# Pooling scores by column tiles, turned by VectorE's block transposes, in a fused attention and maxout kernel

## The chip, the cores and the metric

One core of one Trainium2 chip. The metric is the device time of one execution in microseconds (us). The six runs of the changed kernel lie within 0.2% (341.00 to 341.64 us); the kernel before spreads more (337.8 to 341.4 us over all sessions), and the first experiment says why. Engines: PE is TensorE's matmuls, PEld its weight loads, DVE VectorE, ACT ScalarE, POOL GpSimd, SP the sync engine.

## The reference, cut to what matters

```python
B, N, m, C = 4, 12544, 32, 128
def mab(q, kv):                                  # attention, one head
    s = q @ kv.transpose(0, 2, 1) / sqrt(C)
    a = exp(s - max(s)); a /= a.sum(-1) + 1e-9
    return a @ kv
h = mab(inducing, x)                             # pooling: 32 queries over 12544 rows
y = mab(x, h)                                    # 12544 queries over 32 rows
g = maximum(y @ w1, y @ w2)                      # maxout, 1024 wide
out = g @ w_out
```

A batch has 98 chunks of 128 rows. The pooling of batch b+1 is woven into the main loop of batch b; the first batch's is done at the start.

## The kernel before

The main loop has 196 steps, 49 a batch. A **slot** is one step: a *burst* of row-tiled matmuls into four PSUM banks (L564), their four relus on ScalarE (L599) and VectorE (L595), the 16 output matmuls (L626) of an earlier burst, and the multiply by the softmax denominators on VectorE (L652, called *o*). The program deals its PSUM tiles out to eight banks, and each tile waits for its bank to be read out (in the window of batch 1 shown in the prediction the second L579 matmul starts at 154.71 us, 0.05 us after the last relu of the burst before it has ended). A small cost model in the program picks the engine of each relu. In every other slot, four small matmuls (L579) go ahead into two more banks. `stage` computes the exp of the second attention's scores of a block.

Pooling of the next batch's block i (16 chunks, the seventh has 2):

```python
def p1_scores(b, i):                       # L324: one matmul per chunk, rows in the partitions
    for j in range(n):
        nc.tensor.matmul(out=ps[:, j*M:(j+1)*M], lhsT=xT_tiles[b % 2][:, k0 + j, :],
                         rhs=inducingT, start=True, stop=True)
    nc.scalar.activation(out=et[:, 0:n, :], in_=ps[:, 0:n*M], func=AF.Exp, scale=scale)

def p1_accum(b, i):                        # L346: pooling; the sums of E go to GpSimd
    for j in range(n):
        nc.tensor.matmul(out=ps[:, 0:M], lhsT=xn[:, j, :], rhs=et[:, j, :], ...)
    nc.vector.tensor_add(out=hacc, in0=ps[:, 0:M], in1=hacc)
    nc.gpsimd.tensor_add(out=eacc, in0=eacc, in1=et[:, 0:n, :])

def small_fold(b): ...                     # GpSimd: eacc folded to 32 columns, 4 adds
def small_h(b): ...                        # TensorE sums eacc over partitions, then h
```

The schedule, and the order within a slot:

```python
for i in range(NP1):
    s = g + (14 + 4*i if b == 0 else 5 + 5*i)
    at(s, p1_scores, nb, i)
    at(s + 2, p1_accum, nb, i)
    if nb + 1 < B: at(g + l0 + 2*i, load_x, nb + 1, i)
d = 1 if b == 0 else 0
for s, f in ((40, small_fold), (42, small_h), (43, small_hwd), (44, small_m1)):
    at(g + s + (0 if f is small_fold else d), f, nb)
...
for g, (p, u) in enumerate(seq):
    p.burst(u, lead)
    for blk in stages.get(g, ()): blk.stage()
    if queue: part.final(*a)               # output matmuls, o, and a transfer in every other slot
    for f, *a in jobs.pop(g, ()): f(*a)    # pooling's scores, sums, loads
```

The softmax here doesn't subtract the row's maximum and nothing guards it: scores larger than these inputs give would overflow.

## Time and profile before

| | kernel before |
|---|---|
| time, six runs beside the changed kernel | median 338.86 us (338.05 to 340.41) |
| first profile | span 337.9 us, clock 0.994 |
| PE, DVE, ACT busy | 98%, 88%, 80% |
| plain slot, slot with L579 | 1.329, 1.441 us |
| slot with scores or with pooling | +0.391, +0.390 us |

The slot lengths are the differences between the starts of successive bursts in the timeline of TensorE; nearly all of them repeat to a few ns from execution to execution (a plain slot: 1.328 to 1.330 us; the odd ones are named where they matter), so two kernels can be compared slot by slot. The page's lines that matter are shown and read in the prediction below.

### The profile page before, as it was taken

What the parts mean: (1) busy time and instruction counts of PE and PEld (TensorE: products, weight loads), DVE (VectorE), ACT (ScalarE), POOL (GpSimd) and SP (SyncE); (2) the same over time, 40 slices, a digit from 0 to 9 for tenths busy, and PEclk for the clock granted to TensorE, in tenths of its full rate; (3) what the DMA queues carried; (4) which work ended last, traced back from release to release, by engine and by line L of the source; (5) the groups of instructions that cost most, each with busy time, mean ns of one, the idle gap of its engine ahead of it and who ended that gap; (6) DMA issues with size and microseconds to landing.
All of it is one profiled execution on the core that took longest, in us unless ns stands there. A gap on an engine that the chain in (4) does not pass through costs nothing.

```text
span 337.9 us, 14526 instructions
## 1 busy us (share of the span) xinstructions
PE 330.4 (98%) x6352; PEld 263.9 (78%) x6352; DVE 297.1 (88%) x628; ACT 271.6 (80%) x523; POOL 94.6 (28%) x166
## 2 busy tenths in 40 slices
PE   8999999999999999999999999999999999999995
PEld 3876678888878878888777878888777777878875
DVE  1558999999989999999998999999998998999993
ACT  3748988777898887787898877787899989888881
POOL 6242112275641234543341232332242100000000
PEclk9989999999999999999999999999999999999999
DMA  8999699999929996995229991221221221222222
GB/s 213 209 207 214 171 196 227 196 241 253 262 80 206 222 208 150 175 251 156 79 85 174 258 222 65 97 91 68 96 96 66 108 98 68 95 94 95 96 97 109
DMA packets 54143, 51.47 MB, mean 152 GB/s; under 512 B 41536, under 2 KB 42464, under 8 KB 54080
## 3 DMA queue, kind: packets, MB, share of 16 engines
q0 software_dynamic: 11552, 32.38, 37.6%
q1 hardware_dynamic: 42528, 18.17, 25.4%
q8 instruction: 49, 0.80, 1.0%
q14 instruction: 14, 0.11, 0.1%
HBM read 28.33 MB, written 25.69 MB: 160 GB/s over the span
## 4 chain that ended last, share of the span: by engine, by line
PE 92%; DMA 3%; ACT 2%; DVE 1%; issue 1%; POOL 1%; POOLq 0%
PE ps L626 57%; PE ps L564 19%; PE ps L579 4%; DMA xn<-in_x_dram 3%; PE ps L324 2%; PE ps L346 2%; PE ps L499 2%; ACT relu L599 2%; PE ps L210 1%; PE ps L260 1%; DVE o L652 1%; PE ps L226 1%; PE ps L520 1%; DVE relu L595 1%; PE ps L408 1%
## 5 line engine op out<-in xcount | busy, mean ns | idle before, releaser
L599 ACT ACTIVATE relu<-ps 128x512 f16<-128x512 f32 x445 | 236.0, 601 | 42.1 <-PE ps L564 30.2
L595 DVE TENSOR_SCALAR relu<-ps 128x512 f16<-128x512 f32 x339 | 218.1, 679 | 5.0 <-PE ps L564 4.0
L626 PE MATMUL ps<-woutp,relu 128*128 128x128 f16 x3136 | 208.6, 220 | 0.0
L626 PEld LDWEIGHTS <-relu 128*128 128x128 f16 x3136 | 175.7, 98 | 31.3 <-issue 21.6
L652 DVE TENSOR_TENSOR o<-ps,rp 128x256 f32<-128x256 f32 x196 | 81.8, 417 | 16.3 <-PE ps L626 11.6
L662 POOL DMA_DIRECT2D out_dram<-o x75 | 41.3, 551 | 150.1 <-DVE o L652 102.6
L564 PE MATMUL ps<-e,hwd 32*128 32x256 f16 (+1 forms) x1632 | 82.5, 269 | 0.7 <-ACT relu L599 0.2
L564 PEld LDWEIGHTS <-hwd 32*128 32x128 f16 x1632 | 27.0, 92 | 19.2 <-issue 3.7
L579 PE MATMUL ps<-m,e 32*128 32x128 f16 x372 | 29.8, 214 | 0.8
L579 PEld LDWEIGHTS <-e 32*128 32x128 f16 x372 | 18.3, 92 | 7.1 <-issue 4.2
L366 POOL TENSOR_TENSOR eacc<-eacc,et 128x512 f32<-128x512 f32 (+1 forms) x18 | 18.5, 1029 | 0.3
L333 ACT ACTIVATE et<-ps 128x512 f16<-128x512 f32 (+1 forms) x21 | 11.4, 545 | 5.0 <-PE ps L324 5.0
L120 POOL DMA_DIRECT2D xn<-in_x_dram x21 | 11.4, 545 | 4.9 <-DMA xn<-in_x_dram 1.7
L509 ACT ACTIVATE e<-ps 128x512 f16<-128x512 f32 (+1 forms) x21 | 10.9, 578 | 0.0
L324 PE MATMUL ps<-inducingT,xT 128*128 128x32 f16 x294 | 10.6, 176 | 0.2 <-ACT relu L599 0.2
L346 PE MATMUL ps<-et,xn 128*128 128x32 f16 x294 | 10.6, 176 | 0.0
L215 DVE COPY xT<-ps 128x1024 f16<-128x1024 f16 (+2 forms) x10 | 5.8, 596 | 5.2 <-PE ps L210 5.1
L324 PEld LDWEIGHTS <-xT 128*128 128x128 f16 x294 | 9.5, 96 | 0.4 <-issue 0.4
L346 PEld LDWEIGHTS <-xn 128*128 128x128 f16 x294 | 9.5, 96 | 0.0
L191 PE MATMUL ps<-warm 128*128 128x512 f16 x22 | 7.8, 502 | 1.2 <-DVE warm L167 1.2
L499 PE MATMUL ps<-xT,hT 128*32 128x512 f16 (+2 forms) x120 | 8.8, 353 | 0.0
L210 PE MATMUL ps<-identity,xn 128*128 128x128 f16 x98 | 7.1, 219 | 0.6 <-DMA xn<-in_x_dram 0.3
(79 smaller groups left out, 123.6 us busy)
## 6 DMA issues: line engine op xcount, KB each, us to landing
out_dram<-o POOLq DMA_DIRECT2D x72, 256.0 KB, 3.9
xn<-in_x_dram POOLq DMA_DIRECT2D x21, 512.0 KB, 9.3
out_dram<-o SPq DMA_DIRECT2D x24, 256.0 KB, 2.0
xf<-in_x_dram SPq DMA_DIRECT2D x2, 512.0 KB, 4.2
wf<-in_moe_w_dram SPq DMA_DIRECT2D x2, 512.0 KB, 6.8
xn<-in_x_dram POOLq DMA_DIRECT2D x3, 256.0 KB, 12.0
out_dram<-o POOLq DMA_DIRECT2D x3, 128.0 KB, 4.6
xT<-xn SPq DMA_TRANSPOSE x21, 6.9
```

What stands on the lines that cost most here:

```text
L120: nc.gpsimd.dma_start(out=xn_of(b, i)[:, 0:n, :], in_=xr[b, :, k0 : k0 + n, :])
L324: nc.tensor.matmul(out=ps[:, j * M : (j + 1) * M], lhsT=xT_tiles[b % 2][:, k0 + j, :], rhs=inducingT, start=True, stop=True,)
L346: nc.tensor.matmul(out=ps[:, 0:M], lhsT=xn[:, j, :], rhs=et[:, j, :], start=(j == 0), stop=(j == n - 1),)
L366: nc.gpsimd.tensor_add(out=acc, in0=acc, in1=et[:, 0:n, :])
L499: nc.tensor.matmul(out=ps[32 * q : 32 * (q + 1), 0 : self.width], lhsT=st[self.b]["hT4"][:, 32 * q : 32 * (q + 1)], rhs=xT[:, q % self.g], ...
L564: nc.tensor.matmul(out=ps[:, jj * w : (jj + 1) * w], lhsT=st[blk.b]["hwd"][r, 128 * jb : 128 * (jb + 1)], rhs=blk.e2[r, 128 * self.t0 : 12 ...
L579: nc.tensor.matmul(out=part.fin[q][1][:, 128 * s : 128 * (s + 1)], lhsT=part.blk.e2[r, 128 * tt : 128 * (tt + 1)], rhs=st[part.blk.b]["m1" ...
L595: nc.vector.tensor_scalar(out=dst, in0=src, scalar1=0.0, scalar2=None, op0=ALU.max)
L599: nc.scalar.activation(out=dst, in_=src, func=AF.Relu)
L626: nc.tensor.matmul(out=o, lhsT=self.relu[:, jb, q, tt, :], rhs=woutp[:, jb, :], start=(start and s == 0 and jb == 0), stop=(not start and ...
L652: nc.vector.tensor_mul(self.osb[:, h : h + 2, :], ps[:, 0:256].rearrange("p (s c) -> p s c", s=2), rp.broadcast_to((128, 2, 128)),)
L662: eng.dma_start(out=outr[blk.b, :, k : k + nst, :], in_=self.osb[:, 0:nst, :])
```

## The change

Intent: score a block with four matmuls into four column tiles, side by side (the four L499 matmuls of a round start within 10 ns of each other in the first profile of before, the next round 0.227 us later), in place of 16; do it ahead of the output matmuls so that its exp falls into the lengthened slot; bring E back to rows in the partitions by turning each block of 32 queries by 32 rows on VectorE (one instruction, 0.70 us for 128x512 in the profile after); give turn, pooling and the small steps one slot more; spread a batch's loads over more slots; and finish the start with its smallest unit. The core of the diff:

```diff
+        def col_scores(b, k0, n, name):
+            bi, ps = bank([128, P1B * M])
+            for q in range(4):
+                r = slice(32 * q, 32 * (q + 1))
+                nc.tensor.matmul(out=ps[r, 0 : n * 32], lhsT=inducingT,
+                    rhs=xT_tiles[b % 2][:, k0 : k0 + n, r],
+                    start=True, stop=True, tile_position=(0, 32 * q))
+            eT = eTp.tile([128, P1B * M], F16, name=f"eT_{name}", tag="eT")
+            nc.scalar.activation(out=eT[:, 0 : n * M], in_=ps[:, 0 : n * M], func=AF.Exp, scale=scale)
+            return eT, model.bank_free[bi]
+        def col_turn(eT, ready, n, name):
+            et = etp.tile([128, P1B, M], F16, name=f"et_{name}", tag="et")
+            nc.vector.transpose(et[:, 0:n, :].rearrange("p k m -> p (k m)"), eT[:, 0 : n * M])
+            return et, model.ev("DVE", n * M, ready)
 ... (the start: units 0 to 2 of batch 0 use both; last units in natural order)
-                at(s, p1_scores, nb, i)
-                at(s + 2, p1_accum, nb, i)
+                scores.setdefault(s, []).append((nb, i))
+                at(s + 2, p1_turn, nb, i)
+                at(s + 3, p1_accum, nb, i)
-                    at(g + l0 + 2 * i, load_x, nb + 1, i)
-            d = 1 if b == 0 else 0
-            for s, f in ((40, small_fold), (42, small_h), (43, small_hwd), (44, small_m1)):
-                at(g + s + (0 if f is small_fold else d), f, nb)
+                    at(g + l0 + 3 * i, load_x, nb + 1, i)
+            for s, f in ((41, small_fold), (43, small_h), (44, small_hwd), (45, small_m1)):
+                at(g + s, f, nb)
 ...
                 blk.stage()
+            for b, i in scores.get(g, ()):
+                p1_scores(b, i)
             if queue:
```

"Batch 1", "batch 2" below name the stretch of the main loop (49 slots, counted from 0); the pooling in it is that of the next batch. (The prediction, in "first score of batch 1" and the like, and the expectations name the batch that is pooled; the schedule's slot numbers are the same.)

More of the change, by code (lines that the diff above doesn't have):

```diff
@@ L82 @@
             units.append((i, 0, n))
-    units = units[:-4] + units[-1:] + units[-4:-1]
     NU = len(units)
@@ L89 @@
     etp = ctx.enter_context(tc.tile_pool(name="etp", bufs=7))
+    eTp = ctx.enter_context(tc.tile_pool(name="eTp", bufs=3))
     e2p = ctx.enter_context(tc.tile_pool(name="e2p", bufs=5))
@@ L196 @@
         st = [dict() for _ in range(B)]
+        def col_scores(b, k0, n, name):
+            bi, ps = bank([128, P1B * M])
+            for q in range(4):
+                r = slice(32 * q, 32 * (q + 1))
+                nc.tensor.matmul(
+                    out=ps[r, 0 : n * 32],
+                    lhsT=inducingT,
+                    rhs=xT_tiles[b % 2][:, k0 : k0 + n, r],
+                    start=True,
+                    stop=True,
+                    tile_position=(0, 32 * q),
+                )
+            end = model.pe(32 * n / 2400, model.bank_free[bi], "col")
+            eT = eTp.tile([128, P1B * M], F16, name=f"eT_{name}", tag="eT")
+            nc.scalar.activation(
+                out=eT[:, 0 : n * M], in_=ps[:, 0 : n * M], func=AF.Exp, scale=scale
+            )
+            model.bank_free[bi] = model.ev("ACT", n * M, end)
+            return eT, model.bank_free[bi]
+        def col_turn(eT, ready, n, name):
+            et = etp.tile([128, P1B, M], F16, name=f"et_{name}", tag="et")
+            nc.vector.transpose(
+                et[:, 0:n, :].rearrange("p k m -> p (k m)"), eT[:, 0 : n * M]
+            )
+            return et, model.ev("DVE", n * M, ready)
         pool0 = {}
@@ L223, in u_scores @@
             k = p1_blocks[t][0] + g
+            if i < 3:
+                pool0["et", i], _ = col_turn(*col_scores(0, k, n, f"0_{i}"), n, f"0_{i}")
+                return
             bi, ps = bank([128, P1B * M])
@@ L234, in u_scores @@
             et = etp.tile([128, P1B, M], F16, name=f"et_0_{i}", tag="et")
+            if n % 4:
+                nc.vector.memset(et[:, n : n + 4 - n % 4, :], 0.0)
             nc.scalar.activation(
@@ L249, in u_accum @@
             for j in range(0, n, 4):
-                w = min(4, n - j) * M
                 nc.tensor.matmul(
-                    out=pool0["sum"][1][0:w, 0:1],
-                    lhsT=et[:, j : j + w // M, :],
+                    out=pool0["sum"][1][:, 0:1],
+                    lhsT=et[:, j : j + 4, :],
                     rhs=ones16,
@@ L320, in p1_scores, with p1_turn @@
             k0, n = p1_blocks[i]
-            bi, ps = bank([128, P1B * M])
-            end = 0.0
-            for j in range(n):
-                nc.tensor.matmul(
-                    out=ps[:, j * M : (j + 1) * M],
-                    lhsT=xT_tiles[b % 2][:, k0 + j, :],
-                    rhs=inducingT,
-                    start=True,
-                    stop=True,
-                )
-                end = model.pe(0.025, model.bank_free[bi])
-            et = etp.tile([128, P1B, M], F16, name=f"et_{b}_{i}", tag="et")
-            nc.scalar.activation(
-                out=et[:, 0:n, :], in_=ps[:, 0 : n * M], func=AF.Exp, scale=scale
-            )
-            model.bank_free[bi] = model.ev("ACT", n * M, end)
-            st[b]["et", i] = et, model.bank_free[bi]
+            st[b]["eT", i] = col_scores(b, k0, n, f"{b}_{i}")
+        def p1_turn(b, i):
+            n = p1_blocks[i][1]
+            st[b]["et", i] = col_turn(*st[b].pop(("eT", i)), n, f"{b}_{i}")
         def p1_accum(b, i):
@@ L730 @@
         u_scores(last - 1)
+        u_accum(last - 2)
         u_transpose(last + 1)
-        u_accum(last - 2)
+        u_scores(last)
         u_transpose(last + 2)
-        u_scores(last)
         u_accum(last - 1)
+        u_scores(last + 1)
         u_transpose(last + 3)
-        u_scores(last + 1)
         u_scores(last + 2)
@@ L767 @@
         jobs = {}
+        scores = {}
         def at(g, f, *a):
```

## The prediction

A turn's 0.60 us of VectorE's time, the 0.15 us of a small one and the length of about 0.7 us are the author's estimates in what follows: no run had shown a turn. The first is set equal to a relu of the same 128x512 shape.

> **What bounds the kernel now.** I read the page's parts 1, 2 and 4 first, then the groups of instructions, then the timeline of one stretch, then the start times of all 196 bursts (one burst is the group of L564 matmuls that opens each step of the main loop; "slot" below is the time from one burst's first matmul to the next one's).
>
> ```profile
> span 337.9 us, 14526 instructions
> PE 330.4 (98%) x6352; PEld 263.9 (78%) x6352; DVE 297.1 (88%) x628; ACT 271.6 (80%) x523; POOL 94.6 (28%) x166
> PE 92%; DMA 3%; ACT 2%; DVE 1%; issue 1%; POOL 1%; POOLq 0%
> ```
>
> The second line is busy time, the third the chain of work that ended last. A busy PE need not be a PE at its peak, so the chain matters more: 92% of the span hangs on TensorE's own instructions, 3% (ACT and DVE) on evictions that TensorE had to wait for. Now the groups that the change touches or leans on:
>
> ```profile
> L599 ACT ACTIVATE relu<-ps 128x512 f16<-128x512 f32 x445 | 236.0, 601 | 42.1 <-PE ps L564 30.2 <-ACT relu L599 9.5
> L595 DVE TENSOR_SCALAR relu<-ps 128x512 f16<-128x512 f32 x339 | 218.1, 679 | 5.0 <-PE ps L564 4.0 <-issue 0.2
> L333 ACT ACTIVATE et<-ps 128x512 f16<-128x512 f32 x18 | 10.8, 598 | 5.0 <-PE ps L324 5.0
> L324 PE MATMUL ps<-inducingT,xT 128*128 128x32 f16 x294 | 10.6, 176 | 0.2 <-ACT relu L599 0.2
> L499 PE MATMUL ps<-xT,hT 128*32 128x512 f16 x92 | 7.2, 384 | 0.0
> ```
>
> VectorE has almost no idle time before its relus (5.0 us), ScalarE has 42.1 us before its own: whatever the change puts on VectorE must be paid by handing relus to ScalarE. L324 is the scoring that the change replaces; L499 is a scoring that is already written as the change writes it (four matmuls into four column tiles). A window of the timeline, in batch 1:
>
> ```profile
> 152.38 0.51 PEld L324 LDWEIGHTS <-xT 128*128 128x128 f16 x16
> 152.43 0.56 PE L324 MATMUL ps<-inducingT,xT 128*128 128x32 f16 x16
> 152.92 0.40 PE L564 MATMUL ps<-e,hwd 32*128 32x256 f16 x8
> 153.08 0.60 ACT L333 ACTIVATE et<-ps 128x512 f16<-128x512 f32 x1 [0.40 <-PE ps L324]
> 153.58 2.23 ACT L599 ACTIVATE relu<-ps 128x512 f16<-128x512 f32 x4
> 154.25 0.40 PE L564 MATMUL ps<-e,hwd 32*128 32x256 f16 x8
> 154.48 0.50 PE L579 MATMUL ps<-m,e 32*128 32x128 f16 x4
> 155.91 0.55 PE L346 MATMUL ps<-et,xn 128*128 128x32 f16 x16
> 156.40 0.40 PE L564 MATMUL ps<-e,hwd 32*128 32x256 f16 x8
> ```
>
> Three things are to be seen. The burst at 152.92 starts 0.49 us after the 16 score matmuls start, and a plain slot ends with 0.10 us of switching, so the scores take 0.39 us. The exp of the scores (153.08) lies in front of the next burst's relus on ScalarE, which therefore start only at 153.58. And one slot later TensorE pays for it: L579 takes 0.50 us where it takes 0.27 undisturbed, because it waits for a bank that those late relus still hold. The burst starts give the sizes: a plain slot is 1.329 us (1.441 with L579), in batch 3, which has no pooling, most of the slots are exactly that, and in batches 1 and 2 a score slot is +0.391 and a pooling slot (L346) +0.390. What is above these sums in batches 1 and 2 against batch 3 is +0.20 (slot 12), +0.18 (17), +0.22 (22), +0.25 (32) and about 0.3 in small ones, near 1.1 us a batch. So the main loop is bound by TensorE's issue, with about 1 us of bank stalls a batch that the pooling causes.
>
> [...]below, eight L499 matmuls of 512 columns take two rounds, 124.36 - 123.81 = 0.55 us with the switch, not eight rounds. [...]the first L499 group starts 0.33 us after its burst as L626 would, the two rounds start 0.227 us apart, so 0.55 - 2 x 0.227 = 0.094 us is left for the extra switch.
>
> ```profile
> 123.49 0.40 PE L564 MATMUL ps<-e,hwd 32*128 32x256 f16 x8
> 123.81 0.61 PE L499 MATMUL ps<-xT,hT 128*32 128x512 f16 x8
> 124.36 1.07 PE L626 MATMUL ps<-woutp,relu 128*128 128x128 f16 x16
> 125.36 0.40 PE L564 MATMUL ps<-e,hwd 32*128 32x256 f16 x8
> ```
>
> [...]No run here has shown one. [...]occupying VectorE for about what a relu of 512 does, 0.60 us (its relus last 679 ns and start 598 ns apart when back to back).
>
> **The change part by part.**
>
> *Scores, batches 1 to 3 (18 blocks of 16 chunks, 3 of 2).* Removed: 16 matmuls, 0.391 us. Added: one round of four column tiles, 0.227, plus a switch from row to column tiles to full array, 0.094, sum 0.321. None of the score slots (5, 10, 15 ... and 14, 18, 22 ... in batch 0) coincides with a slot that stages L499, so the switch is paid each time. Saving 18 x 0.07 = 1.26 us. A block of 2 chunks costs 0.041 now; a round of 64 columns plus the switch is about 0.03 + 0.094, so 3 x 0.08 = 0.25 us are lost. Net -1.0 us, all on TensorE, so on the path.
>
> *Turning E on VectorE.* 18 x 0.60 + 3 x 0.15 = 11.3 us more in the main loop. Per batch 3.7 us on a loop of 77.9. Counting starts (relu 0.598 on VectorE, 0.478 on ScalarE, output multiply 0.331), batch 1 occupies VectorE about 71 and ScalarE about 62 of 77.9 us; the sum rises from 85% to 88% of both. It fits, if some six relus a batch go to ScalarE, and the kernel's own balancing counts the turn, so it will. It lies beside TensorE's work: 0 to 0.1 us for a turn that comes before a burst's relus, 0 to 2 us in all.
>
> *Exp earlier.* Scoring now stands between the burst and the output matmuls. Its exp then comes behind the burst's own relus on ScalarE but runs during the lengthened slot (1.65 us against two relus and an exp, 3 x 0.48 = 1.44), and no more in front of the next burst's relus. That should take away half or more of the 1.1 us of stalls in batches 1 and 2; batch 0 shows fewer. Set: -1.5 us in all. Against it, the score needs a bank at the tightest moment: in a slot with L579, four banks of the burst, two of L579 and one waiting for its output multiply leave one.
>
> *Pooling one slot later, loads every third slot, small steps one slot later.* The pooling matmuls are the same. The turn ends slot s+2 and sits in front of the relus of s+3, but that slot is the one lengthened by pooling, so it can absorb it. Loads are hidden: no wait of TensorE, VectorE or ScalarE on a transfer shows in the main loop. I count 0.
>
> *Start (26.0 us to the first burst).* To 13.3 us it waits for x, so the first two units' changes are hidden. After that TensorE runs dense. The third unit's exp ends at 15.93; its turn then takes until about 16.55, while its pooling now starts at 16.16: about +0.4. The turn also delays the copy of unit 4 behind it on VectorE. Having the two-chunk unit last shortens the tail (its exp is 224 ns against 274, and two pooling matmuls fewer follow it): -0.2. Net +0.2.
>
> Sum: 339.3 - 1.0 + 0.7 - 1.5 + 0.2 = 337.7 us.
>
> **The rivals.** *VectorE becomes the bound.* For: it is 88% busy, nearly gapless before relus, and the relus of one burst hold four of eight banks, so 0.6 us at the wrong moment stalls TensorE directly, as the 0.60 us exp does at 153.08. Against: ScalarE has 12 to 13 us idle in each of batches 0 to 2. If each of the 18 turns stalls by 0.2 us and the exp's gain is lost, the result is 339.3 - 1.0 + 3.6 + 0.2 = 342. *Bank wait takes the place of the exp stall.* The early score waits for a relu of the burst before, 0.1 to 0.3 us in half of the blocks: +1 to +3, giving 338.5 to 340. *The stalls vanish entirely.* Both the 1.1 us a batch and some of batch 0's go and the start is unchanged: 339.3 - 1.0 - 3 = 335.3. *Late loads.* In batch 0 the last load now leaves four slots (6 us) before the next batch's transposes are issued, against ten; loads take 9.3 us to land. GpSimd would sit waiting and hold back output transfers; four output buffers are 8 slots, so nothing should reach TensorE.
>
> **Range and chances.** The three runs of before spread over 2.3 us, and my terms that are not read off directly (stalls gained, stalls from turns, start) are each good to about 1.5 us. So 335.4 to 340.3. Faster by over 2% needs 332.5, which would take every stall and more: 4%. Slower needs 346, over 6 us of new stalls: 3%.
>
> **What would show each step right or wrong.** Score slots of 1.65 us for 1.72 (the four matmuls 0.23 us apart from what follows, plus a switch under 0.1): right; 1.72 or more: a bank wait[...]. Turns of about 0.7 us on VectorE, some 18 relus fewer on VectorE and more on ScalarE. L579 back at 0.27 us in the slots after scores. First burst at 26.0 to 26.4 us. Batches 1 and 2 at about 77 us for 77.9, batch 3 unchanged. What would make it wrong: turns twice as long as estimated, or VectorE's idle time gone with TensorE waiting on relus in most pooling slots.

## The result, and the profile after

341.25 us median (341.00 to 341.64, six runs) against 338.86 us for the kernel before in the same rounds. The ratio is 1.0067, 95% interval 1.0041 to 1.0094: within 2%, but slower, where 0.5% faster was forecast and 340.3 was the top of the range. A ratio here is always the mean time of one kernel's fast runs over that of the other's of the same rounds, so not quite the ratio of the medians.

From the page of the kernel after (parts 1, 4 and 5; the burst is now L585, relus L620 and L616, output matmuls L647, o L673, pooling L367):

```profile
span 339.2 us, 14054 instructions
PE 328.3 (97%) x6106; PEld 255.9 (75%) x6106; DVE 299.3 (88%) x634; ACT 280.1 (83%) x542; POOL 94.5 (28%) x166
PE 84%; DMA 5%; DVE 4%; ACT 3%; POOL 2%; issue 1%; POOLq 0%
L620 ACT ACTIVATE relu<-ps 128x512 f16<-128x512 f32 x464 | 245.0, 603 | 40.6 <-PE ps L585 26.4
L616 DVE TENSOR_SCALAR relu<-ps 128x512 f16<-128x512 f32 x320 | 206.3, 678 | 1.9 <-PE ps L585 0.6
L222 DVE STREAM_TRANSPOSE et<-eT 128x512 f16<-128x512 f16 (+1 forms) x24 | 15.4, 640 | 2.9 <-ACT eT L214 2.9
L204 PE MATMUL ps<-xT,inducingT 128*32 128x512 f16 (+1 forms) x96 | 9.0, 365 | 1.0 <-DMA xT<-xn 0.8
```

By the pages TensorE is busy 2 us less. That is not a gain: the first profile of before has a stretch at half clock (next paragraph), and its second profile, without that stretch, shows

```profile
PE 328.1 (97%) x6352; PEld 262.9 (78%) x6352; DVE 297.1 (88%) x628; ACT 271.6 (81%) x523; POOL 94.4 (28%) x166
```

So TensorE's busy time is the same, and the span is longer: in the chain of work that ended last TensorE's share fell from 92% (in both profiles of before) to 84%, and DMA, VectorE, ScalarE and GpSimd took what it lost. 19 relus moved from VectorE (339 to 320) to ScalarE (445 to 464), as forecast.

**A trap in the profile of before.** Stretch by stretch, the first profile of the kernel before has part of its start at half clock, a stretch of 3.41 us from 22.86 us on (the column after the engines' busy times is PEclk):

```profile
20.00:23.00 3.00, 2.46 (x49) 1.91 (x45) 1.02 (x5) 1.14 (x4) 0.98 (x2) 0.98 1.46 202
23.00:26.05 3.05, 3.05 (x24) 1.92 (x20) 1.57 (x3) 1.68 (x4) 0.53 (x1) 0.50 1.07 214
```

In the kernel after, PEclk is 1.00 throughout the start and the first burst starts at 24.70 us, not 26.05. A second profile of the kernel before (first experiment) settles that this is the clock and not the change: 24.69 us, span 336.8. So the fair difference of the traces is 339.2 - 336.8 = 2.4 us, and it lies in the main loop (the medians differ by 2.4 us too, but runs of before with and without the half clock are mixed in them; the first experiment takes them apart):

| slots | before | after | difference |
|---|---|---|---|
| to the first burst (full clock) | 24.69 | 24.70 | 0.0 |
| batch 0 | 76.71 | 78.05 | +1.34 |
| batch 1 | 77.85 | 78.78 | +0.93 |
| batch 2 | 77.93 | 78.78 | +0.85 |
| batch 3 (no pooling) | 70.0 (48 slots) | 70.0 | 0.0 |

(For before, batch 0 is from the second profile of before and batches 1 and 2 from its first; the second had one odd slot in batch 1, 2.35 us for 1.51, which is why the spans differ by 2.4 and this table by 3.1. Batch 0 took 77.18 us in the first profile: slot 14 waited there too, as told below.)

Slot by slot in batch 1 (the same to some hundredths in batch 2), in us:

| slot | what is in it | before | after |
|---|---|---|---|
| 5, 15 | scores | 1.720 | 1.658 |
| 10 | scores and L579 | 1.832 | 1.770 |
| 12 | before: pooling | 2.050 | 1.620 |
| 17 | before: pooling | 1.974 | 1.401 |
| 18 | after: pooling | 1.440 | 2.044 |
| 28 | after: pooling | 1.433 | 2.085 |
| 35 | scores of the 2-chunk block | 1.370 | 1.471 |
| 42 | before: sum of eacc | 1.639 | 1.442 |
| 43 | before: hwd; after: sum of eacc | 1.760 | 2.483 |
| 44 and 45 | before: m1; after: hwd, m1 | 3.235 | 3.631 |

Column tiles do what was forecast (-0.062 us a score slot, +0.101 in the small one). Three things don't. **First, slots 42 to 45 are 0.92 us longer together.** GpSimd's timeline in batch 1, before:

```profile
167.59 0.56 POOL L662 DMA_DIRECT2D out_dram<-o  x1 [2.13 <-DVE o L652]
168.18 2.00 POOL L373 TENSOR_TENSOR eacc<-eacc 128x256 f32<-128x256 f32 x4
170.44 0.56 POOL L662 DMA_DIRECT2D out_dram<-o  x1 [0.26 <-DVE o L652]
```

and GpSimd's and TensorE's after:

```profile
167.15 0.56 POOL L683 DMA_DIRECT2D out_dram<-o  x1 [2.04 <-DVE o L673]
169.97 0.54 POOL L683 DMA_DIRECT2D out_dram<-o  x1 [2.26 <-DVE o L673]
170.52 1.99 POOL L394 TENSOR_TENSOR eacc<-eacc 128x256 f32<-128x256 f32 x4
172.57 0.41 PE L401 MATMUL ps<-eacc,ones 128*128 128x32 f32 x2 [0.75 <-POOL eacc L394]
```

Before, the fold (four adds, 2.0 us) stands in GpSimd's order between two output transfers. After, it was moved by one slot and so landed behind the next transfer, which idles 2.26 us for its o. Measured from the start of slot 40 (166.54 and 166.07 us) the fold starts at 1.64 and 4.45 us: 2.8 us later for a shift of one slot of 1.5 us, because in batches 1 and 2 transfers are issued in odd slots only. TensorE's sum of eacc moved one slot and waits 0.75 us. (In batch 0 the fold alone was moved; it starts 3.36 us after slot 40 before and 3.23 after, and slots 43 to 45 are unchanged.)

**Second, the first score waits for its input**, in TensorE's timeline, batch 0, slot 14:

```profile
44.23 0.40 PE L585 MATMUL ps<-e,hwd 32*128 32x256 f16 x8
45.44 0.40 PE L204 MATMUL ps<-xT,inducingT 128*32 128x512 f16 x4 [0.81 <-DMA xT<-xn]
45.78 1.07 PE L647 MATMUL ps<-woutp,relu 128*128 128x128 f16 x16
```

In front of the output matmuls the score stands 1 us earlier than it did behind them, and its transposed x is still in transit: by the DMA records the block lands 1.08 us after the start of slot 14, and the score starts at 1.21 us. Behind the output matmuls a score comes 1.34 us after the slot's start, so it would not have waited. The DMA records add a second reason: 2 to 3 us after the first transpose is issued, the transposes move 0.014 MB in this profile and 0.21 to 0.22 MB in the same microsecond of both profiles of before. The block lands 6.19 us after that issue; in the second profile of before it took 5.42 us, but 6.70 us in its first, the one with the half clock. There the score of slot 14, behind the output matmuls, waited as well:

```profile
47.27 0.55 PE L324 MATMUL ps<-inducingT,xT 128*128 128x32 f16 x16 [0.23 <-ACT relu L599]
```

The view puts this wait down to a relu (which ends at 47.15 us). But in the second profile of before the same score starts at 45.43 us, before the same relu has ended (45.70), so it doesn't need that one. The block lands at 47.13 us, 0.14 us before the score starts, as in the kernel after (0.13 us): it was the transfer.

**Third, the stalls of the pooling slots did not go away, they moved.** Batch 1, slots 17 and 18, after:

```profile
131.42 0.41 DVE L673 TENSOR_TENSOR o<-ps,rp 128x256 f32<-128x256 f32 x1
131.48 1.07 PE L647 MATMUL ps<-woutp,relu 128*128 128x128 f16 x16
131.75 0.70 DVE L222 STREAM_TRANSPOSE et<-eT 128x512 f16<-128x512 f16 x1
132.38 0.65 DVE L616 TENSOR_SCALAR relu<-ps 128x512 f16<-128x512 f32 x1
132.60 0.55 PE L367 MATMUL ps<-et,xn 128*128 128x32 f16 x16
133.09 0.40 PE L585 MATMUL ps<-e,hwd 32*128 32x256 f16 x8
```

The turn takes 0.70 us behind an o, ends at 132.45, and pooling (L367), for which TensorE was free at about 132.38, starts at 132.60; the burst's VectorE relu is not done until 133.03.

### The profile page after: what moved, and what is told of

Read it like the earlier page. It is cut to its first block, busy times and chain, and to the rows that moved or that the text cites. A ratio compares the mean times of both kernels' runs of the same rounds, so it can differ in the third digit from the quotient of the medians.

```text
span 339.2 us, 14054 instructions
## 1 busy us (share of the span) xinstructions
PE 328.3 (97%) x6106; PEld 255.9 (75%) x6106; DVE 299.3 (88%) x634; ACT 280.1 (83%) x542; POOL 94.5 (28%) x166
## 4 chain that ended last, share of the span: by engine, by line
PE 84%; DMA 5%; DVE 4%; ACT 3%; POOL 2%; issue 1%; POOLq 0%
PE ps L647 53%; PE ps L585 17%; PE ps L600 4%; DMA xn<-in_x_dram 3%; PE ps L367 2%; ACT relu L620 2%; PE ps L204 2%; PE ps L520 2%; DMA xT<-xn 2%; DVE o L673 2%; DVE relu L616 2%; POOL eacc L394 1%; PE ps L239 1%; POOL out_dram L683 0%; PE ps L541 0%
## 5 line engine op out<-in xcount | busy, mean ns | idle before, releaser
L620 ACT ACTIVATE relu<-ps 128x512 f16<-128x512 f32 x464 | 245.0, 603 | 40.6 <-PE ps L585 26.4
L647 PE MATMUL ps<-woutp,relu 128*128 128x128 f16 x3136 | 208.7, 220 | 0.0
L616 DVE TENSOR_SCALAR relu<-ps 128x512 f16<-128x512 f32 x320 | 206.3, 678 | 1.9 <-PE ps L585 0.6
L647 PEld LDWEIGHTS <-relu 128*128 128x128 f16 x3136 | 175.7, 98 | 31.7 <-issue 22.5
L673 DVE TENSOR_TENSOR o<-ps,rp 128x256 f32<-128x256 f32 x196 | 82.0, 419 | 20.7 <-PE ps L647 15.8
L585 PE MATMUL ps<-e,hwd 32*128 32x256 f16 (+1 forms) x1632 | 82.0, 268 | 0.7 <-ACT relu L620 0.2
L585 PEld LDWEIGHTS <-hwd 32*128 32x128 f16 x1632 | 27.1, 92 | 20.0 <-issue 3.2
L600 PE MATMUL ps<-m,e 32*128 32x128 f16 x372 | 28.8, 214 | 0.6
L600 PEld LDWEIGHTS <-e 32*128 32x128 f16 x372 | 18.0, 92 | 6.2 <-issue 3.7
L222 DVE STREAM_TRANSPOSE et<-eT 128x512 f16<-128x512 f16 (+1 forms) x24 | 15.4, 640 | 2.9 <-ACT eT L214 2.9
L214 ACT ACTIVATE eT<-ps 128x512 f16<-128x512 f32 (+1 forms) x24 | 13.6, 565 | 0.1
L367 PE MATMUL ps<-et,xn 128*128 128x32 f16 x294 | 10.5, 176 | 0.6
L367 PEld LDWEIGHTS <-xn 128*128 128x128 f16 x294 | 9.2, 96 | 1.9 <-issue 1.5
L204 PE MATMUL ps<-xT,inducingT 128*32 128x512 f16 (+1 forms) x96 | 9.0, 365 | 1.0 <-DMA xT<-xn 0.8
L191 PE MATMUL ps<-warm 128*128 128x512 f16 x22 | 7.0, 455 | 1.2 <-DVE warm L167 1.2
```

The lines of the kernel that those rows point to most:

```text
L204: nc.tensor.matmul(out=ps[r, 0 : n * 32], lhsT=inducingT, rhs=xT_tiles[b % 2][:, k0 : k0 + n, r], start=True, stop=True, tile_position=(0, ...
L222: nc.vector.transpose(et[:, 0:n, :].rearrange("p k m -> p (k m)"), eT[:, 0 : n * M])
L585: nc.tensor.matmul(out=ps[:, jj * w : (jj + 1) * w], lhsT=st[blk.b]["hwd"][r, 128 * jb : 128 * (jb + 1)], rhs=blk.e2[r, 128 * self.t0 : 12 ...
L600: nc.tensor.matmul(out=part.fin[q][1][:, 128 * s : 128 * (s + 1)], lhsT=part.blk.e2[r, 128 * tt : 128 * (tt + 1)], rhs=st[part.blk.b]["m1" ...
L616: nc.vector.tensor_scalar(out=dst, in0=src, scalar1=0.0, scalar2=None, op0=ALU.max)
L620: nc.scalar.activation(out=dst, in_=src, func=AF.Relu)
```

## The experiments

**The theories.** A: the fold's place in GpSimd's order costs 1.85 us. B (rival of A): slots 42 to 45 are long because turns delay VectorE's part of h. C: the pooling matmuls wait for the turn itself. D (rival of C): the turn takes VectorE's time from the relus, so that banks come free late, and the stall follows it wherever it goes. All runs are of the fast state unless said; "slots" are from the profiles.

### The kernel before once more

No edit.

> The kernel before, unchanged, for a second profile. In its first profile TensorE's clock was halved for 3.4 us just before the first burst, which the profile of the changed kernel doesn't show. Theory: that window hid part of what the changed start costs. Without the window the first burst should start at about 24.3 us (26.05 in the first profile, 24.70 in the changed kernel), and the span be about 336.5 us for 337.9; main-loop slots the same to a few ns. Rival: the changed start really is 1.3 us faster, then the first burst stays at about 26 us at full clock.

One run: 338.54 us, span 336.8, clock 1.000. First burst at 24.69 us.

```profile
20.00:23.00 3.00, 2.45 (x50) 1.92 (x47) 1.00 (x5) 1.14 (x4) 0.89 (x2) 1.00 1.48 204
23.00:24.69 1.69, 1.69 (x24) 1.24 (x22) 1.54 (x3) 1.52 (x4) 0.53 (x1) 1.00 1.04 207
```

Half of the theory holds, that it was the clock: 24 matmuls of the last stretch take 1.69 us at clock 1.00 and 3.05 at 0.50. The other half, that the window hid a cost of the changed start, does not: 24.3 us was expected, and 24.69 us is level with the 24.70 us of the changed kernel. At full clock the changed start neither gains nor loses. Such a window was also in the profile of the fold run on the kernel before, below, and in no other profile.

The window bears on every ratio in this document, since each run's mean clock is on record. Of the 40 runs of the kernel before in the rounds of the experiments, 19 had a clock of 0.998 or more and took 337.77 to 340.61 us (median 338.25); 21 had 0.993 to 0.995, as the two profiles with the window, and took 339.21 to 341.39 us (median 339.96). With the start of before, in its kernel and in three variants, 27 of 58 runs were below 0.998; with the changed start 2 of 66 were (and one more, at 0.950, see below). So at full clock the change is about 3.0 us slower (341.25 against 338.25), which is what the table by slots says, and a kernel with the changed start that is level with before in the ratio is about 1 us slower at full clock. So the changed start seldom meets the window, a gain that the prediction didn't have. Why was not tested. What differs in the profiles is that from 20 to 23 us TensorE is busy 2.15 to 2.47 us in the five with the old start and 2.83 to 2.94 us in the twelve with the changed one.

### Fold back at slot 40

```diff
-            for s, f in ((41, small_fold), (43, small_h), (44, small_hwd), (45, small_m1)):
-                at(g + s, f, nb)
+            d = 1 if b == 0 else 0
+            for s, f in ((40, small_fold), (42, small_h), (43, small_hwd), (44, small_m1)):
+                at(g + s + d, f, nb)
```

> The changed kernel with the small steps of batches 2 and 3 (fold, h, hwd, m1) back at slots 40, 42, 43, 44; batch 1's left at 41, 43, 44, 45. Theory A (fold queued behind an output transfer): at slot 41 the fold stands in GpSimd's order behind the output transfer that only odd slots issue, which waits for that slot's output multiply, so it starts 2.8 us later after slot 40's start for a shift of 1.45 us, and TensorE's sum of eacc waits 0.75 us for it. Then slots 42 to 45 of batches 1 and 2 lose their 0.92 us each, and the time falls by 1.8 us to about 339.4. Rival B (the turn on VectorE delays h's reciprocal and multiply): slots 42 to 45 stay long, time within 0.5 us of 341.25.

339.34 us (339.02 to 339.75), 0.9993 of the kernel before (0.9960 to 1.0025). Slots 42 to 45 of batches 1 and 2 are back at 1.638, 1.760, 1.564 and 1.671, to the ns those of before, and the batches are 0.92 and 0.93 us shorter. GpSimd's timeline:

```profile
167.26 0.56 POOL L683 DMA_DIRECT2D out_dram<-o  x1 [2.04 <-DVE o L673]
167.84 2.00 POOL L394 TENSOR_TENSOR eacc<-eacc 128x256 f32<-128x256 f32 x4
170.08 0.56 POOL L683 DMA_DIRECT2D out_dram<-o  x1 [0.23 <-DVE o L673]
```

Theory A stands, B falls: all turns are still there. (The three full-clock runs of before in these rounds took 338.00 to 338.34 us, so at full clock this kernel is 1.1 us slower than before.)

### The kernel before with the fold at slot 41

```diff
-                at(g + s + (0 if f is small_fold else d), f, nb)
+                at(g + s + (d if b == 0 and f is not small_fold else 0 if b == 0 else 1), f, nb)
```

> The kernel before with one thing of the change: fold, h, hwd and m1 of batches 2 and 3 one slot later (41, 43, 44, 45). Theory A (fold queued behind the output transfer of the odd slot): slots 42 to 45 of those batches grow by 0.92 us each as they do in the changed kernel, the time by 1.85 us over the kernel before. Rival (the fold is late because the last block's pooling is): nothing changes, since the pooling here stays at slot 37.

340.32 us (339.46 to 341.65), 1.0052 of the kernel before (1.0018 to 1.0085), that is +1.8 us. Slots 43 and 44 are 2.496 and 1.866, as in the changed kernel. The late fold costs the same without any of the rest.

### Scores behind the output matmuls

```diff
-                scores.setdefault(s, []).append((nb, i))
+                at(s, p1_scores, nb, i)
```

> The changed kernel with the scores after the output matmuls again, where the kernel before has them; all else as changed. My prediction's view (earlier scores spare the exp stall): the exp comes in front of the next burst's relus again, stalls come back, +1 to +3 us, so 342 to 344. Rival (the earlier place only moved the stalls and brings the first score of batch 0 to the transposes too early): slot 14 of batch 0 loses 0.4 us, the rest stays, so 340.5 to 341.

341.46 us (341.08 to 342.49), 1.0059 of before. In one sum two things cancel: slot 14 of batch 0 falls from 2.54 to 1.66, while batches 1 and 2 grow by 0.31 and 0.46 us. The rest of batch 0 grows by 0.17 us. So the early place is worth 0.2 to 0.5 us a batch in the changed kernel, 0.9 us in all, and in this pair of profiles costs 0.9 once through the first score. (Batch 3 is also 0.27 us longer in this profile, by one odd slot that the edit doesn't touch.) Neither expectation was right about the time.

### First score of batch 1 later

Two forms: behind the output matmuls of slot 14, and one slot later in front of them.

```diff
+                if b == 0 and i == 0: at(s, p1_scores, nb, i)
+                else: scores.setdefault(s, []).append((nb, i))
```

> The changed kernel with one score, the first one of batch 1 in slot 14, behind the output matmuls instead of in front of them. Theory: in front it stands 1 us earlier than in the kernel before and meets its transposed x still in transit (slot 14 took 2.54, 2.67 and 2.84 us in three profiles with the score in front, 1.66 with all scores behind): slot 14 falls to 1.66 to 1.8 us, time falls by 0.8 to 1.0 us, to about 340.3. Rival: the wait only moves to the pooling of slot 17 or to the second score, time within 0.3 us of 341.25.

340.83 us (340.09 to 341.68), 1.0039 of before. Slot 14 was 2.30 in its profile (at another clock, a mean of 0.950): even behind the output matmuls the score waits, if for less. In the run with all scores late it was 1.66, in the two repaired kernels below, which have this edit, 2.25 and 3.26. So the place is not the whole of it; the landing varies too.

```diff
-                s = g + (14 + 4 * i if b == 0 else 5 + 5 * i)
+                s = g + ((15 if i == 0 else 14 + 4 * i) if b == 0 else 5 + 5 * i)
```

> The changed kernel with the first score of batch 1 one slot later (15 for 14), still in front of the output matmuls. Theory (its transposed x lands too late): the wait of 0.9 to 1.2 us in slot 14 goes, 0.5 to 1 us off the time, slot 14 at 1.33. Rival: the wait moves to slot 15 whole, no gain.

340.35 us (339.81 to 341.06), 1.0039 of before. Slot 14 is 1.329 and slot 15 1.969, which is 1.514 + 0.321 for the scores and 0.13 of wait; batch 0 is 0.85 us shorter. The wait is real and is one of timing.

### No turn

```diff
-            nc.vector.transpose(et[:, 0:n, :].rearrange("p k m -> p (k m)"), eT[:, 0 : n * M])
-            return et, model.ev("DVE", n * M, ready)
+            return eT[:, :].rearrange("p (k m) -> p k m", m=M), ready
```

Wrong on purpose: pooling takes unturned weights. It passes the comparison with the reference all the same; with these inputs the scores are of the order of 0.01, every weight is close to 1, and a permutation of them hardly moves the means. So "correct" in the comparison says nothing about the layout of E here.

> The changed kernel without VectorE's transposes: pooling reads the unturned tile, so the result is wrong on purpose. Theory (turn stalls): the 24 turns take 0.70 us each on VectorE and delay the relus of the next burst; the pooling slots then lose about 1 us of waits per batch in batches 0 to 2, and the start about 0.5 us: 337.5 to 338.5. Rival (the turn is hidden beside TensorE's work and the loss is all in the fold and the first score): under 0.7 us, 340.5 to 341.2.

338.83 us (338.32 to 340.44), 0.9983 of before: 2.4 us less than with turns by the medians, 2.8 by the ratios to before. Slots 18 and 28 of batch 1 fall to 1.831 and 1.825, exactly a slot with L579 plus pooling. Batch 1 and 2 are 0.90 and 0.89 us shorter, batch 0 1.07 (its slot 14 put aside), the start 0.26. The turns' total is 2.87 + 0.26 = 3.1 us by the traces.

### Pooling one slot later, turn one slot earlier

```diff
-                at(s + 3, p1_accum, nb, i)
+                at(s + (4 if i < NP1 - 1 else 3), p1_accum, nb, i)
```

> The changed kernel with the pooling of each 16-chunk block one slot later still (4 behind its score, 2 behind its turn). Theory C: the stall is a direct wait, the pooling matmuls wait for the turn, which VectorE runs behind an output multiply, ending 0.2 to 0.3 us after TensorE gets there; then slots 17, 18, 28 and their like lose it, 0.7 to 1 us a batch, in all 2 to 2.7 us, to about 339. Theory D: the turn hurts by delaying relus and so bank frees: then pooling later doesn't help, and the time stays at 341 or rises.

```diff
-                at(s + 2, p1_turn, nb, i)
+                at(s + 1, p1_turn, nb, i)
```

> The changed kernel with the turn one slot earlier (1 behind its score, 2 ahead of the pooling). Theory C: same gain as with the pooling later, 2 to 2.7 us, to about 339, if the turn doesn't delay relus in a plain slot. Theory D: the turn now stands before the relus of a slot that isn't lengthened by pooling, so bank waits appear one slot later: no gain, or a loss up to 1 us.

343.15 (342.61 to 345.44) and 343.74 us (343.27 to 344.37), 1.0114 and 1.0123 of before: both about 2 us *slower* than the change. Theory C alone would have both faster. With the turn earlier, TensorE and VectorE around slot 27 to 28 of batch 1:

```profile
147.08 0.70 DVE L222 STREAM_TRANSPOSE et<-eT 128x512 f16<-128x512 f16 x1
147.70 0.65 DVE L616 TENSOR_SCALAR relu<-ps 128x512 f16<-128x512 f32 x1
147.85 0.40 PE L585 MATMUL ps<-e,hwd 32*128 32x256 f16 x8
148.08 0.59 PE L600 MATMUL ps<-m,e 32*128 32x128 f16 x4
149.51 0.56 PE L367 MATMUL ps<-et,xn 128*128 128x32 f16 x16
```

The turn was issued two slots ahead of its pooling and ends at 147.78, 1.7 us before pooling starts, but it pushed a relu to 147.70 to 148.36; the L600 group (L579 of before) takes 0.59 us for 0.27, its second matmul starting 0.05 us after that relu has ended, which looks like a wait for its bank. Then pooling follows with no turn to wait for. The changed kernel had placed the turn where the slot behind it is lengthened by pooling, and that was the better place of the three.

### Turns executed, but read by nobody

```diff
-            return et, model.ev("DVE", n * M, ready)
+            model.ev("DVE", n * M, ready)
+            return eT[:, :].rearrange("p (k m) -> p k m", m=M), ready
```

Wrong on purpose, as the run without turns.

> The changed kernel with the turns executed as they are but read by nobody: pooling reads the unturned tile (wrong on purpose, as in the run without turns). Theory C (pooling waits for the turn): time and pooling slots as without turns, 338.8, slots 18 and 28 of batch 1 at 1.83 us. Theory D (the turn takes VectorE's time from relus and so delays banks): slots stay near those of the changed kernel, 2.04 and 2.09 us, time near 341.2. A mix shows how much is which.

340.37 us (339.52 to 341.02), 1.0036 of before. This tells C and D apart slot by slot (batch 1):

| slot | with turns | turns unread | no turns |
|---|---|---|---|
| 18 (pooling) | 2.044 | 1.832 | 1.831 |
| 19 | 1.329 | 1.525 | 1.330 |
| 28 (pooling) | 2.085 | 1.825 | 1.825 |
| 29 | 1.875 | 2.126 | 1.876 |
| batch 1 in all | 78.78 | 78.67 | 77.88 |

With nobody waiting for the turn, pooling starts at once, and TensorE loses nearly the same time one slot later: the burst behind the pooling takes 0.59 us for 0.40. Its fourth bank is opened at 132.73 us, 0.06 us after the last two relus of the burst before end, the one behind the turn on VectorE (132.66) and the third one on ScalarE (132.67); so it waits for a bank that a late relu holds.

```profile
131.39 0.70 DVE L222 STREAM_TRANSPOSE et<-eT 128x512 f16<-128x512 f16 x1
132.01 0.65 DVE L617 TENSOR_SCALAR relu<-ps 128x512 f16<-128x512 f32 x1
132.02 0.55 PE L368 MATMUL ps<-eT,xn 128*128 128x32 f16 x16
132.51 0.59 PE L586 MATMUL ps<-e,hwd 32*128 32x256 f16 x8
```

Of the 0.90 us that turns cost batch 1, 0.11 is the wait for the turn and 0.79 is VectorE's time; batch 0, its slot 14 put aside, splits into 0.21 and 0.87. (In the start it is the other way round: with the turns unread the first burst comes at 24.37 us, with none at 24.44, so all of the 0.26 us was a wait.) In the main loop theory D is the main cause; most of the wait of C, visible in the profile, only stands where D's stall would be.

### Turns beside the pooling of the block before

```diff
-                at(s + 2, p1_turn, nb, i)
-                at(s + 3, p1_accum, nb, i)
+                dt, dp = (3, 7 if b == 0 else 8) if i < NP1 - 1 else (2, 3)
+                at(s + dt, p1_turn, nb, i)
+                at(s + dp, p1_accum, nb, i)
```

on top of the fold at slot 40.

> The run with the fold at slot 40, and besides that each turn (but the last small one) issued at the end of a slot that the pooling of the block before lengthens, its own pooling one block later. Theory D (a turn takes VectorE's time from relus, and costs less where TensorE's slot is longer): the stalls of 0.2 to 0.3 us per turn shrink by half or more, 1 to 1.5 us less than the fold run's 339.34, so about 338. Theory C (pooling waits for the turn itself): the turn is then 4 slots ahead of its pooling, so all stalls vanish, about 337. If it isn't faster than 339.3, the place of the turn doesn't matter.

340.19 us (338.85 to 342.68), 1.0051 of before. The pooling slots are free of stalls (18: 1.832, 28: 1.825), but score slots with L579 now stall (10: 1.985 for 1.770, 30: 2.110 for 1.914), and in batch 0 the late last pooling delays the fold (slot 43: 2.307 for 1.630). Batches 1 and 2 gain 0.12 and 0.10 us over the fold run, batch 0 loses 1.05 (0.17 of it in slot 14). The stall moved again.

### Early scores on the kernel before

```diff
-                at(s, p1_scores, nb, i)
+                if b == 0 and i == 0: at(s, p1_scores, nb, i)
+                else: scores.setdefault(s, []).append((nb, i))
```

with the call ahead of the output matmuls, as in the change; row scores, no turns.

> The kernel before, row scores and no turn, with one thing of the change: scores in front of the output matmuls (but for the first of batch 1). My prediction's term for it: exp no more in front of the next burst's relus, pooling stalls of 0.2 us in slots 12, 17, 22, 32 gone, 1 to 1.7 us faster than the kernel before, so about 337. Rival (an early score takes the bank that the next burst needs): no gain, within 0.5 us.

339.70 us (338.94 to 340.72), 1.0030 of before (0.9998 to 1.0061): no gain, also at full clock (339.05 us, the mean of three runs, against 338.24). Slots 12, 17, 22 and 32 of batch 2 lose their stalls (2.05 to 1.82, 1.97 to 1.79, 2.05 to 1.83, 2.15 to 1.93), but slots 10, 20 and 30, where scores meet L579, gain them (1.83 to 1.97, 1.83 to 1.97, 1.83 to 2.18). Slot 10 of batch 2, with VectorE's o in between:

```profile
195.44 0.42 DVE L652 TENSOR_TENSOR o<-ps,rp 128x256 f32<-128x256 f32 x1 [0.16 <-PE ps L626]
195.57 0.27 PE L579 MATMUL ps<-m,e 32*128 32x128 f16 x4
195.91 0.55 PE L324 MATMUL ps<-inducingT,xT 128*128 128x32 f16 x16
```

The score starts 0.34 us after L579, where the group behind L579 starts after 0.21 us in the kernel before, and 0.05 us after o has ended (195.86); slot 20 shows the same. With four banks of the burst and two of L579 taken, the score waits for the bank that o still holds, as the prediction had warned. In slot 30 (here of batch 1; batch 2 is the same) L579 itself waits, 0.61 us for 0.27, its second matmul again starting 0.05 us after o's end (150.30):

```profile
149.77 0.40 PE L564 MATMUL ps<-e,hwd 32*128 32x256 f16 x8
149.88 0.42 DVE L652 TENSOR_TENSOR o<-ps,rp 128x256 f32<-128x256 f32 x1 [0.67 <-PE ps L626]
150.01 0.61 PE L579 MATMUL ps<-m,e 32*128 32x128 f16 x4
150.55 0.56 PE L324 MATMUL ps<-inducingT,xT 128*128 128x32 f16 x16
```

### The start of before

The changed kernel with row scores and the old unit order in the start (the diff's lines for it undone).

> The changed kernel with the start of the kernel before (row scores, no turns, the two-chunk unit ahead of the last three). The first burst starts at 24.69 us in the unthrottled profile of the kernel before, and at 24.70 in the changed kernel, so nothing should change: time 341.0 to 341.5, first burst 24.6 to 24.8 us. Rival: the turns in the start cost 0.26 us (as the run without turns suggests) with no gain from the unit order: 0.2 to 0.3 us faster.

341.92 us (340.82 to 343.36), 1.0077 of before: nothing gained in time. But the trace shows two things. The first burst starts at 25.04 us at full clock, so the changed start is not slower by itself. And slot 14 is 1.854 with the score still in front, 0.2 us of wait for 0.9; batch 0 is 0.71 us shorter than the changed kernel's. (The time doesn't show it: the start is 0.33 us longer, and slot 27 of batch 1 and slot 0 of batch 2 are 0.5 and 0.3 us longer in this one profile.) The DMA records go with this: in the third microsecond after the first transpose's issue, the five profiles with the old start move 0.21 to 0.22 MB of transposes, the twelve with the changed start 0.003 to 0.06 MB. So the pause comes with the changed start. The first block lands 5.42 to 5.60 us after its issue in the three profiles with the old start at full clock, 6.54 and 6.70 us in the two with the half-clock window, and 5.70 to 7.38 us in the twelve with the changed start. One more record goes with the pause: a single packet of 16 KB on the queue marked "instruction" ends 0.3 to 0.6 us after the first transpose's issue with the old start, before any packet of the transposes has, and 2.0 to 2.7 us after it with the changed start, at the head of the pause or in it. That this packet makes the transposes pause is not shown: no run moved it alone.

### The repaired change, and its ceiling

Fold at 40, first score behind the output matmuls, 2-chunk blocks by rows and without a turn, the rest as changed:

```diff
+                if nb == 1 and i == 0 or i == NP1 - 1: at(s, p1_scores, nb, i)
+                else: scores.setdefault(s, []).append((nb, i))
+            if n < 4: (row scores as before, and no turn)
```

> The changed kernel with what the runs so far point to put back: fold at slot 40 in batches 2 and 3, first score of batch 1 behind the output matmuls, and the 2-chunk blocks scored by rows without a turn; column tiles, turns and early scores of all other blocks stay. If the terms add: 341.25 - 1.9 - 0.8 - 0.3 = 338.2, level with the kernel before in its undisturbed runs (338.0 to 338.5).

339.38 us (338.70 to 340.35), 1.0022 of before (0.9991 to 1.0052): level with it in the ratio, 1.2 us slower at full clock (339.47 against 338.24, means), and no better than the fold alone. The terms did not add to the 338.2 us that was expected; slot 14 still took 2.25 us.

The same without turns at all (wrong on purpose; 2-chunk blocks by column tiles):

> No turns (wrong on purpose), fold at slot 40 in batches 2 and 3, first score of batch 1 behind the output matmuls. If the terms add, 338.8 - 1.85 - 0.5 to 0.9 = 336.2 to 336.5: what the change would have been worth with a free turn and the schedule kept. If it is above 337.5, the terms overlap.

336.47 us (335.64 to 337.15), 0.9922 of before (0.9885 to 0.9959). The terms fold and turn add up (338.8 - 1.85 = 337.0); this is about what the change would be worth if turning E were free and the fold in its old place, even with 1.6 us of wait in slot 14: 1.9 us at full clock (336.4 against 338.3, means). No correct version faster than the kernel before was found.

## Why the prediction was wrong

The forecast was 337.7 us, within 2%; it was within 2%, but 3.6 us above the point and 0.9 above the range. (Its sum starts from 339.3 us, a median of three runs that mixes both clocks, and its start of 26.0 us is that of the half-clock window, which it didn't notice; at full clock before takes 338.3 us and its first burst comes at 24.69.) The main-loop terms against the kernel before, by the traces (three batches in all):

| term of the sum | forecast | measured | shown by |
|---|---|---|---|
| scores by column tiles | -1.0 | -0.8 | slots: 18 x -0.062 + 3 x 0.101 |
| small steps one slot later | 0 | +1.85 | fold runs, both ways |
| first score early, its x late | 0 | +0.9 | slot 14: 2.54, 1.66 without a wait (0.8 to 1.4 over seven profiles) |
| turns, main loop | +0.7 | +2.9 | run without turns |
| start, at full clock | +0.2 (turn +0.4, order -0.2) | 0.0 (turn +0.26) | second profile of before |
| exp stalls gone | -1.5 | about -1.7 | what closes the sum; 0.9 of it measured (scores behind) |

**Right.** TensorE bounds the loop (92% of the chain of work before, 84% after); score slots of 1.65 us came out at 1.658; a turn of about 0.7 us by estimate took 698 ns on the mean (128x64, with 0.15 us of VectorE's time in the sum, took 235 ns); about the right number of relus changed engine; batch 3 didn't move.

**Wrong, the step "the small steps one slot later ... I count 0".** It looked at TensorE's slots and not at GpSimd's order. GpSimd issues the output transfers of odd slots (in batches 1 and 2) and waits in order for each one's o. A fold at slot 40 comes between two transfers; at slot 41 it comes behind the second. One slot on TensorE was 2.8 us on GpSimd. The profile of before showed it: 102.6 us of GpSimd's waits are on o, and the fold at 168.18 is followed by a transfer that waits for nothing but 0.26 us.

**Wrong in size, the turns ("0 to 0.1 us for a turn ... 0 to 2 us in all", set at 0.7).** The reasoning was one of averages: VectorE and ScalarE together go from 85 to 88%, so it fits. But a turn must fit between two bursts. The prediction let the slot that pooling lengthens absorb it. With the turns unread slot 18 does take what it takes without them (1.832 against 1.831 us), but the turn stands in front of that burst's last relu, and the next burst waits for a bank that a late relu holds (slot 19: 1.525 for 1.330). So a turn of 0.70 us cost TensorE 0.15 us on average (0.90 us for the six large ones of batch 1), up to 0.26, and moving it, one slot earlier or beside another pooling, moved the stall with it. The first rival of the prediction ("VectorE becomes the bound", 0.2 us a turn) had the size of this. It lost to the argument that ScalarE has idle time; that time was there (ScalarE waits 40.6 us before its relus in the kernel after), but it did not spare these slots the stall.

**Missed, the first score.** The prediction argued that loads are hidden because the kernel before shows no wait on a transfer in its main loop, and counted on that for a score that stands 1 us earlier. The landing of the first transposed block was just hidden in one profile of before (slot 14 1.72) and not in the other, the one that the prediction read (2.11, where the view puts the wait down to a relu). The early place turns a late landing into a wait: with the old start it cost 0.2 us in the one profile of that (1.85), with the changed start 0.8 to 1.4 us in seven profiles (2.47 to 3.09). Behind the output matmuls the changed start gave 1.66, 2.25, 2.30 and 3.26 us. So both add to the wait; why the start does stays open.

**The exp stalls** left their old slots only in part. In batch 1 L579 is back at 0.27 us in slots 32 and 36 (0.50 and 0.48 before), but takes 0.46 and 0.47 us in slots 12 and 22, into which a turn came, and 0.42 us in slot 6, where it took 0.27. Of the -1.7 us, 0.9 is the early place, by the run with the scores behind. Whether the rest is due to pooling a slot later or to column tiles holding TensorE for less time stays open. On the kernel before the early place gained nothing, because in slots with L579 it met a bank that o still held.

## What to carry to other kernels

Moving a step by one slot of the bounding engine can move it on another engine's queue by whatever stands in between (here 1.5 us on TensorE became 2.8 us on GpSimd): before calling such a shift free, write down what it now comes behind on each queue. When two engines drain a ring of buffers close to the pace of the producer, extra work on one of them must fit between two fillings, not into the batch's average (here a turn of 0.70 us cost TensorE 0.15 us on average, with VectorE busy for 72.3 and ScalarE for 68.2 of the 78.78 us of batch 1); a stall seen in front of one consumer is worth removing only if a run with the result unread shows the time goes with it. Compare profiles slot by slot, and check the granted clock, of the stretch and of every run, before believing a difference or a ratio.
